# A Fourier block and a gated feed-forward block on one core: half of the last copies put behind the first token products, and one table load moved back in its queue

## The chip, the cores and the metric

The kernel runs on one core of a Trainium2 chip. The metric is the device time of one execution in microseconds, as the median over several runs. A profile comes from one separate, profiled execution, whose own time stands beside it. The engines are called PE (matrix products), ACT, DVE and POOL (element-wise work), and SP, which here only issues transfers. POOL issues transfers as well as computing, and an engine takes its instructions strictly in the order in which they stand in its queue.

## The reference, cut to what matters

The input x has 2048 tokens of 576 features in bf16.

```
def _A_ref(x, w_r, w_i):
    X = rfft2(x.astype(float32), axes=(-2, -1))
    X = X * (w_r + 1j * w_i)
    return irfft2(X, s=(S, D), axes=(-2, -1)).astype(bfloat16)

def _B_ref(x, w_gate, w_up, w_down):            # 576 -> 4608 -> 576
    return (gelu(x @ w_gate) * (x @ w_up)) @ w_down

h  = x + _A_ref(_layernorm(x), w_r, w_i)
h2 = h + _B_ref(_layernorm(h), w_gate, w_up, w_down)
```

The two-dimensional transforms are computed as products with tables of cosines and sines. The second part, three products with 4608 wide weights, is most of the arithmetic.

## The kernel before, in words

Tokens lie as 16 tiles of 128 rows: tile c holds the rows 16p + c. The work has three stretches.

The first stretch loads x, takes the statistics of the first layer norm, and makes the forward transform over the rows into U.

The second stretch runs over 16 groups of frequencies, in an order that is written out by hand in `SEQF` (line 28). For a group i, `st_D` transforms along the features, `st_B` finishes the forward transform, `st_T` multiplies by the filter on DVE, and `st_V` begins the inverse transform on PE. Its result, 256 columns in each of two banks, is copied into the tile V by ACT or DVE, or by one engine for each bank (`VENG`, line 29). The last 32 frequencies of every group, the tail, do not go through `st_V`: `st_R` collects the tails of four groups (a quarter q, from 0 to 3) and makes their inverse in one go. For the quarters 0 to 2 the result goes into RB by one copy and from there, because partitions have to change, by eight small transfers into the tile VR; they are dealt out over the queues of SP and POOL (`r0` to `r2` are their semaphores). For quarter 3 it goes straight from the accumulator into VR by eight copies of 32 partitions, four on ACT and four on DVE. The last group is number 15 (`LAST`), and its product and the tail product of quarter 3 close the stretch: `... V15 R3 v15 r3`. A capital letter is the first half of a product, a small one the second half, with the copies that follow.

The third stretch is ordered by `SEQ` (line 35). `I`/`i` (`i_mm`) is the inverse transform along the features of one token tile c: its first half needs V of every group, its second half V and VR of every group. `E` (`i_ev`) copies the result to GS, `N`/`o` (`n_mm`) makes the last inverse step with the table IT, `a` (`x_add`) adds it to x on DVE, `s`, `q`, `c` take the statistics of the second layer norm, `n` (`norm`, line 885, always with the letter P: on POOL) writes the normalised tile into HN, `u`/`U` (`turn_mm`, line 901) transposes it on PE with the table IDT, `e` copies it to HT, and `G0`, `G1` begin the products with the gate and up weights (`gu_part`, line 935). Only the token tiles 0 to 7 (`NPRE`) are done there. The tiles 8 to 15 are deferred: `def_i` and `def_n` (lines 991 and 1011) do them between the weight products of the first 512 tokens, from the third of these on. A product takes one of four pairs of accumulator banks; which pair is free, and so what a product waits for, comes from a small loop above `i_mm` that replays `SEQ`.

After that the kernel is one long row of weight products: gate and up products for 512 tokens at a time (line 948), then the down products (line 1048).

Transfers are issued by SP and POOL in program order. The loads of tables and of the filter come first on SP, in this order at their end: DT (the table of `i_mm`), IT (512 KB, the table of `n_mm`), IDT (32 KB), then four small filter loads of `w_zero`; behind them stand the VR transfers of the quarters. The first slot of the weights is loaded on SP in twelve parts, `a0` to `a5` and `b0` to `b5`, each behind a `hold`, a wait for the last PE instruction before it in the program (`LOADS`, line 31).

Of the kernel before, what the change touches and what calls it, by code (L numbers as in the profile page):

```python
# [15 lines left out]
NT = 16  # L16
# [14 lines left out]
LOADS = {".I0": "a0 a1 a2 a3 a4 a5", ".N0": "b0", ".i3": "b1", ".o1": "b2", ".N3": "b3", ".o3": "b4 b5", ".i7": "d"}  # L31
# [3 lines left out]
SEQ = """I0 I1 I2 i0 E0S i1 E1S i2 E2A N0 I3 o0 i3 N1 I4 o1 a0 E3S N2 o2 a1 s0A q0 i4 a2 s1A I7 c0 N3 E4S q1 s2D i7 I6 o3 E7A i6 c1 N4 o4 a3 q2 E6A c2 N7 I5 o7 a4 n0P N6 s3A a7 i5 n1P n2P q3 c3 o6 u1 U1 u2 E5A u0 U2 a6 n3P e1A e2D U0 N5 u3 e0A o5 a5 U3 G0 e3D G1""".split()  # L35
# [11 lines left out]
def build_tables():  # L47
# [107 lines left out]
    T["VTAB"] = np.stack([v if k else v.reshape(128, 4, 16, 4).transpose(0, 1, 3, 2).reshape(128, 256) for v, k in ((VN[0, 0], 1), (VN[0, 0], 0), (VN[1, 0], 1), (VN[1, 1], 1), (VN[1, 0], 0), (VN[1, 1], 0))], 1).reshape(128, -1)  # L155
# [176 lines left out]
def _build(nc, A_x, A_w_r, A_w_i, B_w_gate, B_w_up, B_w_down, out):  # L332
# [20 lines left out]
    VR = sb.alloc("VR", [128, NG, 2, 4, NT], BF16)  # L353
# [58 lines left out]
    RB = sb.alloc("RB", [128, 3, 2, 2, 4, NT], BF16)  # L412
# [20 lines left out]
    P.op(POOL, lambda g: g.memset(VR[:, :, :, :, :], 0.0), w=[("V", g, 2 + t) for g in range(NG) for t in range(2)])  # L433
# [51 lines left out]
    P.dma(SP, IT[:, :, :, :].rearrange("p a b c -> p (a b c)"), dram["ITAB"][:, :], "it", w=["IT"])  # L485
    P.dma(SP, IDT[:, :], dram["EYE"][:, :], "eye", w=["IDT"])
# [199 lines left out]
    def st_V(i, second, engs):  # L686
        g, z, b0 = GORD[i], i % NZ, FB["V", i]

        def mm(h, o, ct, first, last, after):
            c, t_ = ct  # L690
            return P.op(PE, lambda t: t.matmul(bank(b0 + o, 0, 128, 128 * c, 128 * c + 128), TP[64 * h:64 * h + 64, z, o, t_, c:256:2], VT[64 * h:64 * h + 64, 0 if g else 2 + o, t_, :],  # L691
                                               start=first, stop=last), r=[("T", z), "VT" if g else "VT2"], w=[("PS", b0 + o)], after=after)

        halves(("V", i), second, [[(c, t_) for c in range(2) for t_ in range(2)]] * 2, mm)
        if not second:
            return
        v5 = V[:, :, :, :, g, :, :].rearrange("p c t n j e -> p j (c t n) e")
        n = 2 // len(engs)
        for a, e in enumerate(engs):
            ev(e, v5[:, n * a:n * a + n], banks(b0 + a, n, 256).rearrange("p a (c e) -> p a c e", e=4), [("PS", b0 + a + k) for k in range(n)], [("V", g, a + k) for k in range(n)])  # L700

    def st_R(q, second):
# [12 lines left out]
        if q < 3:  # L715
            ev(RENG[q], RB[:, q, :, :, :, :].rearrange("p t o e n -> p o t (e n)"), banks(b0, 2, 128).rearrange("p o (t x) -> p o t x", t=2), keys, [("RB", q)])
            for j, i in enumerate(js):
                for t_ in range(2):
                    k = t_ if q == 2 else (2 * j + t_) % 3 > 0
                    P.dma((SP, POOL)[k], VR[64 * t_ + 32 * (j % 2):64 * t_ + 32 * (j % 2) + 32, GORD[i], :, :, :], RB[32 * j:32 * j + 32, q, t_, :, :, :], f"r{q}{k:d}", r=[("RB", q)], w=[("V", GORD[i], 2 + t_)])  # L720
            return
        for i in js:
            j, g = i % 4, GORD[i]
            for t_ in range(2):
                dst = VR[64 * t_ + 32 * (j % 2):64 * t_ + 32 * (j % 2) + 32, g, :, :, :].rearrange("p o e n -> p o (e n)")
                src = PS[32 * j:32 * j + 32, b0 * 512:(b0 + 2) * 512].rearrange("p (a c) -> p a c", a=2)[:, :, 128 * (i == LAST) + 64 * t_:128 * (i == LAST) + 64 * t_ + 64]
                ev((ACT, DVE, DVE, ACT)[j], dst, src, keys, [("V", g, 2 + t_)])
# [36 lines left out]

    def tab2_load():
# [13 lines left out]
    def loads(w):  # L779
        for v in LOADS.get(w, "").split():  # L780
            if v == "d":
                tab2_load()
# [27 lines left out]
    vkeys = vmain + vtail  # L810


    SLOT, last, held, ing = {}, [sorted(used.values()).index(used[2 * b]) - 4 for b in range(4)], set(), False
    for t, w in enumerate(SEQ):
# [6 lines left out]
        elif k in "ioUEae":  # L821
            b = SLOT[{"i": "I", "o": "N", "U": "u", "E": "I", "a": "N", "e": "u"}[k], i] // 2
            if k in "Eae":
                held.discard(b)
            else:
                last[b] = t + 1
        elif k == "G":
# [5 lines left out]
    def i_mm(c, second):  # L833
        b, e = SLOT["I", c], ends.setdefault(("I", c), [None, None])
        for j in range(2 + second):
            for r in range(2):
                o, r0 = r ^ (not second), 64 * r
                lhs = V[r0:r0 + 64, j, o, c, :, :, :] if j < 2 else VR[r0:r0 + 64, :, :, :, c].rearrange("p g o e -> p (g o e)")
# [121 lines left out]
    def gu_first(i):  # L960
        for a in range(4):
# [5 lines left out]
           "e": turn_ev, "G": gu_first}  # L967
# [18 lines left out]
    fdead = ["DT", "IT", "J0", "J1", "ZD"] + [(n_, c) for n_ in ("ATB", "ATS") for c in range(NT)] + [("G", i // 2, i % 2) for i in range(10)] + [*[("Y", a) for a in range(NY)], *[("RB", a) for a in range(3)]]  # L986
# [4 lines left out]
    def def_i(c, second):  # L991
        e = ends.setdefault(("X", c), [None, None])
        for j in range(3):
            for r in range(2):
                o, r0 = r ^ (not second), 64 * r
                t_ = j if j < 2 else r
                lhs, rhs = (V[r0:r0 + 64, o, t_, c, :, :, :], DP[r0:r0 + 64, 2 * o + t_, :]) if j < 2 else (VR[r0:r0 + 64, :, :, :, c].rearrange("p g o e -> p (g o e)"), DP[r0:r0 + 64, 4 + o, :])
                e[o] = P.op(PE, lambda t, o=o, t_=t_, lhs=lhs, rhs=rhs, j=j: t.matmul(bank(6 + o, 0, 128, HK * t_, HK * t_ + HK), lhs, rhs, start=(not second and j == 0), stop=(second and j == 2)),  # L998
                            r=vk[o if j < 2 else 2] + ["DP"], w=[("PS", 6 + o)], after=[e[o]] if second and j == 0 else [])
# [134 lines left out]
```

## Time and profile before

| what | value |
|---|---|
| runs, us | 486.0, 485.41, 485.42; median 485.42 |
| profiled execution: its own time / the span of the instructions | 484.82 us / 483.0 us |
| PE busy | 476.7 us, 99% of the span |
| DVE, ACT, POOL busy | 183.2, 145.4, 51.2 us |
| granted PE clock | full speed in all of the 40 slices |
| gate and up products (lines 948, without and with WGX) | 233.4 + 53.4 us |
| down products (line 1048) | 133.0 us |
| end of the second stretch to the first weight product | 42.2 us to 54.3 us of the span |

The profiled execution is 1.8 us longer than its span; what lies around the span is taken as unchanged. The page counts a matmul as busy until a modelled end, so gaps of PE shorter than about 0.3 us show in the starts of its matmuls more than in its busy time. The stretch that the change touches is short, from about 24 us to 59 us; the 420 us after it are products back to back.

### The profile page before, as it was taken

The numbers are of one execution on the slowest core, as the hardware profiler recorded it, in microseconds if no ns is written. First come the engines' busy times: TensorE is split into PE (matmuls) and PEld (weight loads), VectorE is DVE, ScalarE is ACT, GpSimd is POOL, SyncE is SP. The second block draws the span as 40 slices with busy tenths as digits, with TensorE's granted clock in tenths as the row PEclk, the third lists the DMA queues.
The fourth block names the chain that finished last, engine by engine and source line by source line (L and its number), as shares of the span: only waits on it lengthen the run. The fifth ranks groups of instructions, "written<-read, shape, count | busy, mean of one in ns | idle before, by whom it ended". The sixth has DMA issues, their size and how long they took to land.

```text
span 483.0 us, 12887 instructions
## 1 busy us (share of the span) xinstructions
PE 476.7 (99%) x5873; PEld 289.0 (60%) x5874; DVE 183.2 (38%) x366; ACT 145.4 (30%) x291; POOL 51.2 (11%) x86
## 2 busy tenths in 40 slices
PE   7999999999999999999999999999999999999998
PEld 3877755555588644444688544444788444445884
DVE  7998655565500143333200244333101233333011
ACT  6998753434300022332100122233000232223000
POOL 7753317010120000000000000000000000000000
PEclk9999999999999999999999999999999999999999
DMA  8883878951520001000000011000000000000000
GB/s 292 226 219 70 278 248 289 375 104 27 195 88 17 26 18 23 18 1 0 3 14 15 26 24 23 12 0 2 3 14 27 14 1 0 1 1 1 3 26 26
DMA packets 28454, 33.19 MB, mean 69 GB/s; under 512 B 12656, under 2 KB 21488, under 8 KB 28400
## 3 DMA queue, kind: packets, MB, share of 16 engines
q1 hardware_dynamic: 24768, 19.88, 14.6%
q0 software_dynamic: 3632, 12.49, 7.9%
q8 instruction: 46, 0.75, 0.7%
q14 instruction: 8, 0.07, 0.0%
HBM read 26.21 MB, written 2.36 MB: 59 GB/s over the span
## 4 chain that ended last, share of the span: by engine, by line
PE 96%; DVE 1%; DMA 1%; POOL 1%; issue 0%; SPq 0%; POOLq 0%; DVEq 0%
PE PS L948 58%; PE PS L1048 27%; PE PS L650 2%; PE PS L1060 2%; PE PS L691 2%; PE PS L561 1%; DMA XO<-in_A_x_dram 1%; PE PS L670 1%; PE PS L839 1%; PE PS L998 1%; DVE XO L862 1%; PE PS L1015 0%; PE PS L856 0%; POOL XN L577 0%; POOL ATS L530 0%
## 5 line engine op out<-in xcount | busy, mean ns | idle before, releaser
L948 PE MATMUL PS<-HT,WG 64*128 64x512 bf16 (+1 forms) x2142 | 233.4, 372 | 0.1
L948 PEld LDWEIGHTS PS<-HT,WG 64*128 64x128 bf16 x2142 | 109.2, 94 | 111.1 <-DMA WG<-in_B_w_up_dram 0.2
L956 ACT ACTIVATE GL<-PS 128x512 bf16<-128x512 f32 x144 | 85.7, 596 | 281.8 <-PE PS L948 281.8
L957 DVE TENSOR_TENSOR AT<-GL,PS 128x512 bf16<-128x512 bf16 x144 | 98.8, 687 | 166.0 <-ACT GL L956 166.0
L1048 PE MATMUL PS<-WD,AT 64*128 64x288 bf16 x2160 | 133.0, 283 | 0.0
L1048 PEld LDWEIGHTS PS<-WD,AT 64*128 64x128 bf16 x2160 | 107.9, 94 | 25.2
L1035 DVE TENSOR_TENSOR OS<-PS,XO 128x288 bf16<-128x288 f32 (+2 forms) x32 | 13.2, 452 | 125.5 <-PE PS L1048 118.0
L948 PE MATMUL PS<-HT,WGX 64*128 64x512 bf16 x486 | 53.4, 376 | 0.0
L948 PEld LDWEIGHTS PS<-HT,WGX 64*128 64x128 bf16 x486 | 24.3, 94 | 28.2
L865 ACT ACTIVATE OS<-XO,NM 128x576 bf16<-128x576 bf16 x15 | 11.6, 773 | 11.4 <-DVE XO L1019 11.4
L650 PE MATMUL PS<-FT,U 64*128 64x288 bf16 x160 | 13.3, 283 | 0.0
L683 DVE TENSOR_TENSOR TP<-YS,WS 128x1024 bf16<-128x1024 bf16 x16 | 11.0, 686 | 0.9 <-DMA WS<-WS 0.6
L504 DVE BATCH_NORM_STATS2 ST<-XO 128x6 f32<-128x288 bf16 x26 | 10.1, 440 | 2.0 <-DMA XO<-in_A_x_dram 2.0
L691 PE MATMUL PS<-VT,TP 64*128 64x128 bf16 x256 | 10.0, 217 | 0.0
L242 POOL DMA_DIRECT2D WG<-in_B_w_gate_dram x9 | 6.1, 679 | 34.4 <-DMA WG<-in_B_w_gate_dram 31.0
L572 ACT ACTIVATE U<-PS 128x384 bf16<-128x384 f32 (+2 forms) x27 | 9.4, 485 | 0.7 <-PE PS L561 0.7
L561 PE MATMUL PS<-ATS,XO 128*128 128x128 bf16 x96 | 8.1, 219 | 1.5 <-POOL ATS L530 1.5
L242 POOL DMA_DIRECT2D WD<-in_B_w_down_dram x9 | 6.7, 755 | 23.8 <-PE PS L1015 23.8
L616 ACT ACTIVATE CUS<-PS 128x576 bf16<-128x576 f32 x14 | 9.0, 656 | 0.3 <-PE PS L650 0.2
L1060 PE MATMUL PS<-WD,AT 128*128 128x448 bf16 (+1 forms) x72 | 9.0, 286 | 0.0
L616 ACT ACTIVATE YS<-PS 128x576 bf16<-128x576 f32 x14 | 8.9, 657 | 0.3
L691 PEld LDWEIGHTS PS<-VT,TP 64*128 64x128 bf16 x256 | 7.9, 94 | 1.4 <-DVE V L616 0.2
(89 smaller groups left out, 227.9 us busy)
## 6 DMA issues: line engine op xcount, KB each, us to landing
WD<-in_B_w_down_dram POOLq DMA_DIRECT2D x9, 576.0 KB, 12.1
WG<-in_B_w_up_dram SPq DMA_DIRECT2D x6, 576.0 KB, 7.1
WG<-in_B_w_gate_dram POOLq DMA_DIRECT2D x6, 576.0 KB, 6.3
out_dram<-OS SPq DMA_DIRECT2D x30, 72.0 KB, 1.7
XO<-in_A_x_dram SPq DMA_DIRECT2D x6, 288.0 KB, 4.8
WGX<-in_B_w_up_dram SPq DMA_DIRECT2D x2, 576.0 KB, 4.4
WGX<-in_B_w_gate_dram POOLq DMA_DIRECT2D x2, 576.0 KB, 5.5
HT<-HN SPq DMA_TRANSPOSE x60, 2.4
```

Of the source, the lines that this page charges most:

```text
L242: fn = lambda e: e.dma_start(out_ap, in_ap)
L561: P.op(PE, lambda t, b=b, lhs=lhs, p0=p0, p1=p1, s=s, e=e, o=o, c=c: t.matmul(bank(b, p0, p1, o, o + 128), lhs, ATS[:, c, :], start=s, sto ...
L616: fn = (lambda v: v.tensor_copy(dst, src)) if eng == DVE else (lambda a: a.activation(dst, src, ACTF.Copy))
L650: return P.op(PE, lambda t: t.matmul(bank(b0 + o, 0, 128, 0, 2 * HK), U[64 * h:64 * h + 64, us, 2 * i:2 * i + 2, :, :], FT[64 * h:64 * h + ...
L691: return P.op(PE, lambda t: t.matmul(bank(b0 + o, 0, 128, 128 * c, 128 * c + 128), TP[64 * h:64 * h + 64, z, o, t_, c:256:2], VT[64 * h:64 ...
L865: P.op(ACT, lambda a, c=c, out=out: a.activation(out, XO[:, c, 0:D], ACTF.Square, bias=NM[:, c:c + 1], accum_out=SB2[:, 1, c:c + 1]), r=[( ...
L948: op = P.op(PE, lambda t, h0=h0, kt=kt, wt=wt, b=b, s=(not second and j == 0), e=(second and j == n - 1): t.matmul(bank(b, 0, 128, c0, c1) ...
L956: P.op(ACT, lambda a: a.activation(GL[:, s2, :], bank(b0), ACTF.Gelu_apprx_tanh), r=[("PS", b0)], w=[("GL", s2)])
L957: P.op(DVE, lambda v: v.tensor_tensor(AT[:, f, :], GL[:, s2, :], bank(b0 + 1), op=ALU.mult), r=[("GL", s2), ("PS", b0 + 1)], w=[("AT", f)])
L1035: P.op(DVE, lambda v: v.tensor_tensor(OS[:, p % 2, d0:d1], bank(b, 0, 128, 0, d1 - d0), XO[:, c, d0:d1], op=ALU.add), r=[("PS", b), ("X", ...
L1048: e[h] = P.op(PE, lambda t, f=f, h=h, r0=r0, j=j: t.matmul(bank(b0 + h, 0, 128, 0, 288), AT[r0:r0 + 64, f, 128 * p:128 * p + 128], WD[r0:r ...
L1060: P.op(PE, lambda t, b=b, d0=d0, d1=d1, f=f, j=j: t.matmul(bank(b, 0, 128, 0, d1 - d0), AT[:, f, 128 * p:128 * p + 128], WD[:, f, d0:d1], ...
```

## The change

There are four edits.

1. The copies that close the second stretch are cut in two by token tiles. The token index of V and VR is split into tiles 0 to 7 and tiles 8 to 15. For group 15 (`v_half`) each engine first copies the half for tiles 0 to 7, 128 columns in place of 256. For quarter 3 the eight copies into VR take 64 columns in place of 128, the tiles 0 to 7. The other half of group 15 is copied by the new entry `l15`, which stands behind `i0`. The other half of quarter 3 is copied by the new entry `l3` (`tail_late`), behind `I3`: one copy of 96 partitions on ACT and one of 32 partitions on DVE into RB, and then eight transfers of 4 KB from RB to VR, all on the queue of POOL (semaphore `rl`). The products of the deferred tiles wait for all of these; those of the tiles 0 to 7 wait only for the first halves.
2. `SEQ` changes at its head: `I2` moves behind `i0`, since its banks are those of group 15, which are held until `l15`. The bank loop counts the banks of group 15 and of quarter 3 as held until `l15` and `l3`.
3. The loads of IT and IDT leave their place in front of the four loads of `w_zero` and stand on SP behind the VR transfers of quarter 1 (`"r1": "t"` in `LOADS`).
4. VR gets a layout with the two halves of the tiles apart, so a transfer writes two runs of 64 elements to a partition in place of one of 128. The 24 transfers of the quarters 0 to 2 are dealt out anew: SP issues 5, 5 and 4 of them and POOL 3, 3 and 4, where it was 3, 3, 4 and 5, 5, 4. One table has its columns in another order to match.

```diff
-LOADS = {".I0": "a0 a1 a2 a3 a4 a5", ...
+LOADS = {"r1": "t", ".I0": "a0 a1 a2 a3 a4 a5", ...
-SEQ = """I0 I1 I2 i0 E0S i1 E1S i2 E2A N0 I3 o0 i3 N1 I4 o1 a0 E3S ...
+SEQ = """I0 I1 i0 l15 E0S I2 i1 E1S i2 E2A N0 I3 l3 o0 i3 N1 I4 o1 a0 E3S ...
...
-    VR = sb.alloc("VR", [128, NG, 2, 4, NT], BF16)
+    VR = sb.alloc("VR", [128, 2, NG, 2, 4, NT // 2], BF16)
...
-    P.dma(SP, IT[:, :, :, :].rearrange("p a b c -> p (a b c)"), dram["ITAB"][:, :], "it", w=["IT"])
-    P.dma(SP, IDT[:, :], dram["EYE"][:, :], "eye", w=["IDT"])
...
+        if i == LAST:
+            v_half(i, 0, ("V", g))
+            return
...
+    def v_half(i, k, key):
+        for a, e in enumerate((ACT, DVE)):
+            src = bank(FB["V", i] + a, 0, 128, 0, 256).rearrange("p (q x) -> p q x", q=4)[:, :, 32 * k:32 * k + 32].rearrange("p q (n e) -> p q n e", e=4)
+            ev(e, V[:, :, :, 8 * k:8 * k + 8, GORD[i], a, :].rearrange("p c t n e -> p (c t) n e"), src, [("PS", FB["V", i] + a)], [(*key, a)])
...
-                    k = t_ if q == 2 else (2 * j + t_) % 3 > 0
+                    k = t_ ^ (j % 2) if q == 2 else (2 * j + t_) % 3 == 1
...
+    def tail_late(q, engs):
+        b0 = FB["R", 3]
+        for p0, p1, c, e in ((0, 96, 0, engs[0]), (96, 128, 128, engs[1])):
+            ev(ENG[e], RB[p0:p1, 0, :, 1, :, :].rearrange("p t o x -> p o t x"), PS[p0:p1, b0 * 512:(b0 + 2) * 512].rearrange("p (a c) -> p a c", a=2)[:, :, c:c + 128].rearrange("p a (t x) -> p a t x", t=2)[:, :, :, 32:64],
+               [("PS", b0), ("PS", b0 + 1)], [("RB", 0, p0)])
+        for i in range(12, 16):
+            for t_ in range(2):
+                j = i % 4
+                P.dma(POOL, tail_place(i, t_, 1), RB[32 * j:32 * j + 32, 0, t_, 1, :, :].rearrange("p o x -> p (o x)"), "rl", r=[("RB", 0, 96 if i == LAST else 0)], w=[("VL", GORD[i], 2 + t_)])
...
+    def it_load():
+        P.dma(SP, IT[:, :, :, :].rearrange("p a b c -> p (a b c)"), dram["ITAB"][:, :], "it", w=["IT"])
+        P.dma(SP, IDT[:, :], dram["EYE"][:, :], "eye", w=["IDT"])
...
+    vlate = [("VM", GORD[LAST], a) for a in range(2)] + [("VL", GORD[i], 2 + t) for i in range(12, NG) for t in range(2)]
...
-                            r=vk[o if j < 2 else 2] + ["DP"], w=[("PS", 6 + o)], after=[e[o]] if second and j == 0 else [])
+                            r=(vk[o] if j < 2 else vtail) + vlate + ["DP"], w=[("PS", 6 + o)], after=[e[o]] if second and j == 0 else [])
```

41 lines of the change are left out of this document (23 added, 18 removed).

## The prediction

> **What bounds the kernel now.** I read the page first: PE is busy for 99% of the span at the full clock, and the chain that ended last is PE for 96% of it. So almost all of the time is products the change does not touch, and it can only act through the moment at which the weight products begin. Then I read the chain of waits from the end of the second stretch to that moment.
>
> ```profile
> 42.17 0.42 DVE V L616
> 42.60 0.14 issue
> 42.73 1.16 PE PS L839 x16
> 43.89 0.06 issue
> 43.95 1.08 PE PS L839 x14
> ...
> 45.86 0.76 DVE XO L862
> ...
> 50.19 0.67 DVE XO L862
> 50.86 0.05 issue
> 50.91 0.42 PE PS L839 x4
> ...
> 54.27 0.06 issue
> 54.33 0.70 PE PS L948 x9
> ```
>
> PE waits for the copy of group 15 into V (to 42.73), then for the copies into VR (to 43.95), later for DVE's additions (to 50.91), and the weight products begin at 54.33. Next the timelines of DVE and POOL.
>
> ```profile
> 42.16 0.42 DVE L616 CAST V<-PS 128x256 bf16<-128x256 f32 x1
> 42.62 1.19 DVE L616 CAST VR<-PS 32x128 bf16<-32x128 f32 x4
> ...
> 39.23 1.96 POOL L242 DMA_DIRECT2D VR<-RB  x4 [0.27 <-ACT RB L616]
> 48.64 0.86 POOL L890 TENSOR_SCALAR HN<-XO,NM,RS 128x640 bf16<-128x640 bf16 x1 [7.45 <-DVE RS L875]
> 50.30 0.87 POOL L890 TENSOR_SCALAR HN<-XO,NM,RS 128x640 bf16<-128x640 bf16 x1 [0.80 <-DVE RS L875]
> 51.34 0.87 POOL L890 TENSOR_SCALAR HN<-XO,NM,RS 128x640 bf16<-128x640 bf16 x1 [0.17 <-POOL HN L890]
> 52.54 0.87 POOL L890 TENSOR_SCALAR HN<-XO,NM,RS 128x640 bf16<-128x640 bf16 x1 [0.32 <-DVE RS L875]
> ```
>
> The reader is to see two things: DVE's copies on the path are half a microsecond and less, and POOL, which looks idle from 41.2 to 48.6, makes the four normalised tiles of the first 512 tokens one behind the other until 53.41. PE transposes the last of them from 53.61 on, 0.20 us after POOL ends, and 0.7 us later the weight products begin. Last the transfers.
>
> ```profile
> IT<-c_itab SPq DMA_DIRECT2D x1, 512.0 KB, 6.1
> VR<-RB SPq DMA_DIRECT2D x10, 8.0 KB, 3.0
> WG<-in_B_w_up_dram SPq DMA_DIRECT2D x1, 112.0 KB, 6.3
> ```
>
> The last weight part leaves SP at 52.01 and lands 6.3 us later, at 58.3. The 72 matmuls with the first 256 weight columns run from 54.33 with one start every 0.055 us, to 58.3 as well. So starting them earlier, without earlier weights, brings nothing.
>
> **The front (edits 1 and 2).** DVE's copies of 256 and 512 columns take 0.42 and 0.68 us, so a column costs 0.001 us: 128 columns 0.29, 64 columns about 0.22 (an estimate from these rows; the 128-column VR copies take 0.285). PE starts 0.13 earlier, at 42.60. I0, I1 and i0 are 12 matmuls at 0.061 a start, to 43.34. The VR copies, four at 0.22 with 0.014 between them from 42.48, end at 43.41, and PE starts 0.15 after such an end (42.58 to 42.73 in the rows): 43.56, where it was 43.95. But now I2 has still to come (0.25 us), and it waits for DVE's second half of group 15, 0.29 us behind the VR copies: 43.71, PE at 43.86. So i1 begins at 44.10, before it was 44.11: nothing is left. Then a small loss: I3 now takes the banks of token 1, whose copies on DVE end at 45.13, so it starts at 45.28, where it stood at 45.16. That moves DVE's first addition from 45.86 to 45.98, and DVE has no gap from there to 50.86. The front is worth between -0.13 (the start alone) and +0.12; I take +0.12 at 50.9, and it stays behind what follows. The l3 copies cost about 0.27 (ACT) and 0.29 (DVE), in gaps of 0.53 and 0.73 us in front of ACT's 46.25 and DVE's 45.86; without that cover they would add that much.
>
> **POOL's eight new transfers (edit 1).** ACT's l3 copy runs behind the copy that ends at 45.72, to 45.93. POOL started its transfers of quarter 2 0.29 us after the copy they read (38.95 to 39.23), so here at 46.2. It issues one in 0.49 us (x4 in 1.96), whatever DVE does meanwhile (DVE was 100% busy from 39 to 41): eight take 3.9 us, to 50.1. The four normalisations are queued behind them. They take 0.87 with 0.17 between two: they end at 51.0, 52.1, 53.1 and 54.1, where they ended at 49.5, 51.2, 52.2 and 53.4. The first two are not yet awaited: PE transposes tile 1 from 52.26. Tile 2 reaches PE at 53.30 in place of 52.7, tile 3 at 54.34 in place of 53.61. What follows tile 3 is o5, U3 and the weight products: 0.44 us of starts and about 0.1 more, so 54.87. Before, the last 0.2 us went to ACT's copy of tile 0, which now ends at 54.7 and is not last. The weight products start +0.54 late. Bounds: a POOL issue at the dearest row of its kind, 0.59 us for the filter copies at 32.3, adds 8 x 0.10 = 0.8; with normalisations without a gap it is 0.4 less. I take the middle, since the VR rows are the nearest.
>
> **The weights.** They hang on SP's holds; the first is for I0, about 0.13 earlier. They land at 58.2 to 58.6 (the 32 KB of late VR data are 0.1 us at the 280 GB/s worked out below; up to 0.3 if their small packets cost more), before PE needs them at 58.8. The 0.05 us that PE may lose to them now is gone.
>
> **The tables on SP (edits 3 and 4).** Four w_zero loads leave 0.96 us earlier (two issues of 0.44 with their steps). POOL's filter copies waited 2.67 us for one of them to 32.3, and DVE waited 0.45 and 0.20 us for such copies; PE stands back to back there, so I count nothing, between -0.4 and 0. SP issues five r1 transfers from 33.89 (0.5 to 0.6 each, one of 1.25 as in every quarter) to 37.6, IT and IDT to 38.55, and reaches r2 at 38.97, as before. IT, by its 6.1 us, is there by 43.8, and its first reader comes at 44.9; IDT's comes at 52.3. The r2 transfers now stand behind 544 KB: they landed by 43.4 and are needed at 43.5. At 280 GB/s, which the b parts show (448 KB every 1.6 us), IT's data take 1.9 us and are gone by about 41.6, so the last two, issued at 40.2 and 41.5, land as before. Runs of 128 bytes in place of 256 double small packets and I count nothing for them, at most 0.1 us. The wait on rl before the deferred products costs nothing: the last lands by 52.7 (1.6 to 2.6 after issue on POOL), they start at 60.5.
>
> **Sum.** +0.54 - 0.05 = +0.5 us. On the profiled execution's 484.82 that is 485.3. The median of the runs is 0.6 above it, at 485.42; the same step gives 485.9.
>
> **Rivals.** (1) Slower by more than a measurement can tell: r2 lands late. In the trace r0, with the queue full, took 4.6 us to land and more, r2 with it empty 2.4 to 3.0. If the full-queue price holds for the last r2 transfer, or r2 waits for IT's 6.1 us (43.8 to 44.2, plus their own time), the products with VR start at 44.6, 1.05 late, and so does l3 with POOL's row behind it: +0.5 + 1.0, 486.9. It decides once the last r2 lands after 43.5. Against it: small w_i loads issued at 25.58, behind IT, landed at 29.2, before IT's 30.7. [...] (2) POOL's issues cost 0.59 or more: +0.5 + 0.8 = +1.3, 486.7. (3) POOL's row is hidden, as when its issues overlap or PE finds other work: then the front decides, from 0.13 earlier to 0.12 later, and weights that land at 58.2 cap the gain: 485.3. With up to 0.4 from the earlier filter copies, 485.0.
>
> **How the numbers follow.** A change under 0.2% (0.97 us) can hardly be told from none. Forecast 0.60, rival 1 0.12, rival 2 0.12, rival 3 0.16. The forecast is inside the bound but for 0.03 of its chance on the slow side, rivals 1 and 2 are outside on the slow side in all but 0.02, rival 3 is inside but for 0.03 on the fast side. So faster 0.03, same 0.72, slower 0.25. The likeliest alone lies between 485.5 and 486.3; the range runs from rival 3's front case to rival 1, with 0.1 for the spread of runs: 485.1 to 486.9.
>
> **What would show it.** In the profile after: PE's first V product near 42.6 and its first VR product near 43.55; a wait of PE before I2 and before I3; eight POOL issues from 46.2 to 50.1 and the normalisations shoulder to shoulder behind them, the last ending near 54.1; PE waiting for HN between 52.8 and 54.3; the first weight product near 54.9. I am wrong if POOL's row does not delay the last normalisation, if the first VR product waits for a transfer, or if the second stretch itself changes length by more than 0.3 us.

## The result, and the profile after

The changed kernel takes 488.79 us (median of 11 executions, 487.26 to 489.77). The kernel before, run beside it, takes 485.75 us (11 executions, 484.95 to 486.97). The ratio is 1.0056, with a 95% interval from 1.0042 to 1.0070. So it is slower by about 2.7 us by the ratio (3.0 between the medians), where the forecast was +0.5 with a range up to +1.5.

The profiled execution has a span of 486.9 us (before 483.0) and its own time is 488.72 us. From the third weight product to the end the kernel takes 424.8 us (before 424.7), so the whole loss lies in front of it. The chain of waits of the changed kernel (start, duration, what), from the transfers of quarter 2 to the first weight product, with the numbers of its own lines (L866 is `i_mm`, L883 `n_mm`, L889 `x_add`, L935 `turn_mm`, L975 the weight products):

```profile
40.31 0.60 SPq L242
40.90 0.04 issue
40.95 3.77 DMA VR<-RB
44.71 0.46 issue
45.17 1.40 PE PS L866 x18
46.57 0.48 PE PS L883 x4
47.05 0.48 PE PS L866 x4
...
50.04 1.49 DVE XO L889 x2
...
53.27 0.66 DVE XO L889
53.94 0.05 issue
53.98 0.42 PE PS L866 x4
...
57.34 0.77 DVE XO L889
58.11 0.14 issue
58.24 6.31 PE PS L975 x92
```

Three things are new in it. The first VR product starts at 45.17 (before 43.95) and waits for a transfer of quarter 2 that was issued at 40.95 and landed at 44.71; that is one of the signs by which the prediction wanted to be called wrong. From 46.57 on, four products take 0.48 us, where most rows of four of before have 0.24 to 0.26. And the first weight product, at 58.24 in place of 54.33, waits for an addition of DVE that ends at 58.11. The waits of PE (us in total, times, longest) say the same:

```profile
PE PS L866 <- DMA VR<-RB: 2.0, 1, 2.0
PE PS L975 <- DVE XO L889: 0.9, 1, 0.9
```

Next the timelines of DVE and POOL after the change (start, us, work, idle time before it and what ended that):

```profile
42.13 0.92 DVE L614 CAST VR<-PS 32x64 bf16<-32x64 f32 x4
43.08 0.29 DVE L614 CAST V<-PS 128x128 bf16<-128x128 f32 x1
...
47.71 3.94 POOL L242 DMA_DIRECT2D VR<-RB  x8 [6.71 <-ACT RB L614]
51.72 0.87 POOL L917 TENSOR_SCALAR HN<-XO,NM,RS 128x640 bf16<-128x640 bf16 x1
53.38 0.87 POOL L917 TENSOR_SCALAR HN<-XO,NM,RS 128x640 bf16<-128x640 bf16 x1 [0.80 <-DVE RS L902]
54.43 0.88 POOL L917 TENSOR_SCALAR HN<-XO,NM,RS 128x640 bf16<-128x640 bf16 x1 [0.17 <-POOL HN L917]
55.62 0.88 POOL L917 TENSOR_SCALAR HN<-XO,NM,RS 128x640 bf16<-128x640 bf16 x1 [0.31 <-DVE RS L902]
```

The eight new issues take 3.94 us, as forecast, but 1.5 us later, and the second and the last normalisation wait for DVE's RS, as they did before: DVE is so late here that the row on POOL decides nothing. The transfers between 38 and 47 us (bytes each, median time from issue to landing):

```profile
IT<-c_itab SPq DMA_DIRECT2D x1, 512.0 KB, 3.9
...
VR<-RB POOLq DMA_DIRECT2D x4, 8.0 KB, 2.9
VR<-RB SPq DMA_DIRECT2D x4, 8.0 KB, 3.2
```

The transfers of VR in the same stretch of before, and one window of 3.41 us of before (busy time of PE, PEld, DVE, ACT and POOL, granted clock, DMA share, GB/s):

```profile
VR<-RB POOLq DMA_DIRECT2D x6, 8.0 KB, 1.9
VR<-RB SPq DMA_DIRECT2D x4, 8.0 KB, 2.7
```

```profile
42.88:46.29 3.41, 3.35 (x54) 2.56 (x52) 2.13 (x7) 2.08 (x7) 0.00 (x0) 1.00 0.47 124
```

Three windows of the same length after, the first in the same place:

```profile
42.88:46.29 3.41, 1.40 (x24) 1.15 (x20) 1.07 (x4) 0.86 (x4) 0.00 (x0) 1.00 0.60 159
46.29:49.70 3.41, 3.41 (x33) 2.67 (x30) 1.72 (x4) 2.03 (x5) 1.99 (x5) 0.50 0.47 126
49.70:53.11 3.41, 3.30 (x50) 2.13 (x46) 3.07 (x5) 2.41 (x8) 2.82 (x5) 1.00 0.89 274
```

After the window with the wait, in which PE was busy for 1.40 of 3.41 us (before 3.35), the granted clock is 0.50 for 3.41 us, and then full again. Of the 11 executions three kept the full clock throughout (487.26, 487.32 and 487.37 us); eight had a mean granted clock of 0.996 or 0.997 and took 487.92 to 489.77, with a median of 488.88.

So the 3.91 us by which the first weight product is late are made up, in the profiled execution, of -0.49 (PE's first V product at 42.24, before 42.73), +1.71 (from there to the VR product, 2.93 in place of 1.22) and +2.69 (from there to the first weight product, 13.07 in place of 10.38). The experiments take these apart.

### The profile page after: what moved, and what is told of

Same layout as the page of the kernel before. It is cut to its first block, busy times and chain, and to the rows that moved or that the text cites. A ratio compares the mean times of both kernels' runs of the same rounds, so it can differ in the third digit from the quotient of the medians.

```text
span 486.9 us, 12902 instructions
## 1 busy us (share of the span) xinstructions
PE 478.3 (98%) x5874; PEld 342.7 (70%) x5874; DVE 184.0 (38%) x368; ACT 145.5 (30%) x293; POOL 52.8 (11%) x90
## 4 chain that ended last, share of the span: by engine, by line
PE 94%; DMA 1%; POOL 1%; DVE 1%; ACT 1%; issue 1%; SPq 0%; POOLq 0%; DVEq 0%
PE PS L975 58%; PE PS L1075 27%; PE PS L1087 2%; PE PS L648 2%; PE PS L559 1%; PE PS L866 1%; DMA VR<-RB 1%; PE PS L689 1%; DMA XO<-in_A_x_dram 1%; PE PS L883 1%; PE PS L1025 1%; DVE XO L889 1%; PE PS L668 1%; ACT YS L614 1%; POOL XN L575 0%
## 5 line engine op out<-in xcount | busy, mean ns | idle before, releaser
L975 PE MATMUL PS<-HT,WG 64*128 64x512 bf16 (+1 forms) x2142 | 233.7, 372 | 0.9 <-DVE XO L889 0.9
L975 PEld LDWEIGHTS PS<-HT,WG 64*128 64x128 bf16 x2142 | 131.1, 94 | 90.4 <-issue 1.0
L1075 PEld LDWEIGHTS PS<-WD,AT 64*128 64x128 bf16 x2160 | 132.3, 94 | 0.7
L975 PE MATMUL PS<-HT,WGX 64*128 64x512 bf16 x486 | 53.6, 376 | 0.0
L975 PEld LDWEIGHTS PS<-HT,WGX 64*128 64x128 bf16 x486 | 29.9, 94 | 22.5
L242 POOL DMA_DIRECT2D VR<-RB x18 | 9.2, 521 | 11.1 <-ACT RB L614 11.1
```

Source lines behind the costliest of these rows:

```text
L242: fn = lambda e: e.dma_start(out_ap, in_ap)
L975: op = P.op(PE, lambda t, h0=h0, kt=kt, wt=wt, b=b, s=(not second and j == 0), e=(second and j == n - 1): t.matmul(bank(b, 0, 128, c0, c1) ...
L1075: e[h] = P.op(PE, lambda t, f=f, h=h, r0=r0, j=j: t.matmul(bank(b0 + h, 0, 128, 0, 288), AT[r0:r0 + 64, f, 128 * p:128 * p + 128], WD[r0:r ...
```

## The experiments

All times are ratios to the kernel before, run on the same chip beside each, with 95% intervals. "V", "VR" and "first weight product" are starts on PE in the profiled execution.

### The late transfers: one table move, one dealing

**The table move alone**: the kernel before with edit 3.

```diff
-LOADS = {".I0": "a0 a1 a2 a3 a4 a5", ".N0": "b0", ".i3": "b1", ".o1": "b2", ".N3": "b3", ".o3": "b4 b5", ".i7": "d"}
+LOADS = {"r1": "t", ".I0": "a0 a1 a2 a3 a4 a5", ".N0": "b0", ".i3": "b1", ".o1": "b2", ".N3": "b3", ".o3": "b4 b5", ".i7": "d"}
-    P.dma(SP, IT[:, :, :, :].rearrange("p a b c -> p (a b c)"), dram["ITAB"][:, :], "it", w=["IT"])
-    P.dma(SP, IDT[:, :], dram["EYE"][:, :], "eye", w=["IDT"])
...
+    def it_load():
+        P.dma(SP, IT[:, :, :, :].rearrange("p a b c -> p (a b c)"), dram["ITAB"][:, :], "it", w=["IT"])
+        P.dma(SP, IDT[:, :], dram["EYE"][:, :], "eye", w=["IDT"])
```

> The kernel before with edit 3 alone: IT and IDT behind the transfers of quarter 1 on SP. Theory A: r2 lands after 44, PE's first VR product moves from 43.95 to about 45, the kernel is 1 us slower, and 1.5 us more in executions where the clock drops (ratio 1.002 to 1.005). Theory B: r2 lands by 43.4 as before, no change beyond 0.2 us (ratio 1.000).

Measured: 485.16 us, ratio 0.9996 (0.9987 to 1.0005), all ten executions at full clock. IT is issued at 35.94 and landed at 39.91. The last r2 lands at 43.19 and VR starts at 43.76, the first weight product at 54.14. So the table move by itself neither costs nor gains, as theory B has it: an early r2, as before, and a start 0.19 us earlier, which a later wait of 0.9 us for a weight part takes back.

**Everything but the table move**: the changed kernel with edit 3 undone.

```diff
-LOADS = {"r1": "t", ".I0": "a0 a1 a2 a3 a4 a5", ".N0": "b0", ".i3": "b1", ".o1": "b2", ".N3": "b3", ".o3": "b4 b5", ".i7": "d"}
+LOADS = {".I0": "a0 a1 a2 a3 a4 a5", ".N0": "b0", ".i3": "b1", ".o1": "b2", ".N3": "b3", ".o3": "b4 b5", ".i7": "d"}
...
+    P.dma(SP, IT[:, :, :, :].rearrange("p a b c -> p (a b c)"), dram["ITAB"][:, :], "it", w=["IT"])
+    P.dma(SP, IDT[:, :], dram["EYE"][:, :], "eye", w=["IDT"])
```

> The changed kernel with edit 3 alone undone: IT and IDT are loaded again in front of the filter loads of w_zero; the copies in halves, the late row on POOL, the new layout and the new dealing stay. Theory A (the r2 transfers are late because they stand behind IT and IDT in SP's queue): r2 lands by about 43.4, PE waits less than 0.3 us before the first VR product instead of 2.0, the granted clock stays full, and what is left over the kernel before is the row on POOL and the wait of the first weight product for the last addition, about +1.5 us (ratio 1.003). Theory B (r2 is late because its transfers have twice as many runs and are dealt out anew): nothing changes, the wait stays at 2 us and the ratio near 1.0056.

Measured: 487.16 us, ratio 1.0041 (1.0027 to 1.0056), six executions at full clock (486.68 to 487.43) and two below it (488.33, 488.37). IT landed at 31.35, the last r2 lands at 43.89, and VR starts at 44.35, behind a wait of 0.5 us where theory A allowed 0.3. Most of the loss is still there, though r2 is only half a microsecond late. So r2 is not the only cause; the wait of 0.88 us in front of the first weight product is here too (56.38).

**The old dealing**: the changed kernel with SP 3, 3, 4 and POOL 5, 5, 4 transfers, as before.

```diff
-                    k = t_ ^ (j % 2) if q == 2 else (2 * j + t_) % 3 == 1
+                    k = t_ if q == 2 else (2 * j + t_) % 3 > 0
```

> The changed kernel with the dealing of the 24 tail transfers as it was (SP 3, 3, 4 and POOL 5, 5, 4); tables behind quarter 1, halves, layout and the late row on POOL stay. Theory F (neither edit alone but both: five transfers of quarter 1 on SP instead of three hold IT back by about 2 us, so that its data run into r2's): IT leaves SP near 36 and not near 38, r2 lands about 0.9 us after PE's first V product (2.5 in the changed kernel), the first VR product follows 0.46 us behind that, the clock drops in few executions or none, and the kernel is 1.0 to 1.5 us slower than the one before (ratio 1.002 to 1.003). Theory G (the halved runs and the layout make r2 late by themselves once a table is near): r2 still lands 2 us or more after the first V product and the ratio stays above 1.004.

Measured: 486.88 us, ratio 1.0032 (1.0020 to 1.0044), seven executions at full clock and three below. With two r1 transfers fewer on SP, IT is issued at 36.71 in place of 37.92, and that is enough: r2 lands at 43.22, and VR starts at 43.67. What remains is the forecast's row on POOL, to the tenth, and a wait behind it that the forecast did not have. From the chain of waits of this kernel:

```profile
50.12 0.88 POOL HN L917
...
51.17 0.88 POOL HN L917
...
52.21 0.89 POOL HN L917
...
53.26 0.89 POOL HN L917
54.14 0.14 issue
54.28 0.26 PE PS L935 x6
54.54 0.26 PE PS L883 x4
54.80 0.02 issue
54.83 0.77 DVE XO L889
55.59 0.14 issue
55.73 4.33 PE PS L975 x45
```

The normalisations end at 51.0, 52.1, 53.1 and 54.1. The weight products could start at 54.85 (forecast 54.87), but wait 0.88 us for DVE's last addition. This execution is one of the three below full clock; the half clock comes late in it, from 55.95 to 59.36, so that the third weight product follows the first after 5.59 us in place of 3.93.

**Table or dealing**: two runs for the question that these three leave open, whether IT's data do it, the five transfers on SP, or the order inside SP's queue. In the first the changed kernel keeps its dealing and loads IT behind quarter 0. In the second it has the old dealing, and IT stands behind the first r2 transfer on SP.

```diff
-LOADS = {"r1": "t", ".I0": "a0 a1 a2 a3 a4 a5", ".N0": "b0", ".i3": "b1", ".o1": "b2", ".N3": "b3", ".o3": "b4 b5", ".i7": "d"}
+LOADS = {"r0": "t", ".I0": "a0 a1 a2 a3 a4 a5", ".N0": "b0", ".i3": "b1", ".o1": "b2", ".N3": "b3", ".o3": "b4 b5", ".i7": "d"}
```

```diff
-LOADS = {"r1": "t", ".I0": "a0 a1 a2 a3 a4 a5", ".N0": "b0", ".i3": "b1", ".o1": "b2", ".N3": "b3", ".o3": "b4 b5", ".i7": "d"}
+LOADS = {".I0": "a0 a1 a2 a3 a4 a5", ".N0": "b0", ".i3": "b1", ".o1": "b2", ".N3": "b3", ".o3": "b4 b5", ".i7": "d"}
...
                     k = t_ if q == 2 else (2 * j + t_) % 3 > 0
...
+                    if (q, j, t_) == (2, 0, 0):
+                        it_load()
```

> The changed kernel with IT and IDT behind the transfers of quarter 0 in place of those of quarter 1; the dealing of 5, 5 and 4 on SP stays. IT is then issued near 33.8, and its data are gone by about 38, before r2 begins. Theory (r2 is late because IT's data move while r2 is under way): the last r2 lands at 43.2 to 43.9, PE's first VR product 0.46 later, the time 1.003 to 1.004 of the kernel before, as with the old dealing (486.5 to 487). Rival (five and five on SP make r2 late, whatever IT does): the last r2 lands near 44.7 and the time stays at 1.0055.

> The changed kernel with the old dealing (3, 3 and 4 on SP), and IT and IDT issued behind the first of the four r2 transfers on SP, so near 39.3 to 40.3. POOL's four r2 transfers are issued from 38.9 to 41.0 as ever, on a queue that holds nothing of the tables. Theory (IT's data hold up whatever is under way beside them): POOL's last r2 lands at 44.3 or later where it landed at 42.88 with the old dealing, SP's at 44.7 or later, VR near 45.2, time 1.005 or more. Rival (the order within SP's queue does it): POOL's last lands at 42.9, and only SP's three come late.

Measured, first: 487.14 us, ratio 1.0038 (1.0025 to 1.0051); the last r2 lands at 43.25 and VR starts at 43.71, with the new dealing. Second: 488.33 us, ratio 1.0059 (1.0040 to 1.0078); SP's last r2 lands at 44.99, POOL's last at 44.31, VR starts at 45.45. The transfers of the second from 38.5 us on:

```profile
IT<-c_itab SPq DMA_DIRECT2D x1, 512.0 KB, 4.7
...
VR<-RB SPq DMA_DIRECT2D x4, 8.0 KB, 2.4
VR<-RB POOLq DMA_DIRECT2D x4, 8.0 KB, 3.3
```

and the same stretch of the first, with IT's data gone before:

```profile
VR<-RB SPq DMA_DIRECT2D x4, 8.0 KB, 2.6
VR<-RB POOLq DMA_DIRECT2D x4, 8.0 KB, 2.0
```

So r2 is late where IT's data move while it is under way, on whichever queue it stands: POOL's four, issued from 38.9 to 41.0 on a queue that holds no table, take 3.3 us in place of 2.0. The dealing matters in the changed kernel only because it holds IT back by 1.2 us. In the packets of the changed kernel the last 128 bytes of r2 start at 42.97 us and the semaphore comes 1.7 us later, at 44.71; with the old dealing the last starts at 42.86 and lands at 43.22.

The lateness hangs on a few updates. The trace has 16 updates of the semaphore for each transfer. Of the 64 for SP's four r2 transfers in the changed kernel, 60 had come by 43.39, where the kernel with the table behind quarter 0 had all 64 by 43.25; the last four came at 43.67, 44.19, 44.53 and 44.71. In that kernel and with the old dealing one packet of 16 KB with instructions moves from 40.09 to 41.05 and from 40.01 to 41.00; in the changed kernel it moves from 41.31 to 42.25, directly behind IT's data. Whether this packet, the first weight packets at 43.75 or something else holds the last four updates isn't shown.

### The wait in front of the weight products

**Other banks**: the changed kernel, with two products on each other's banks. The bank loop takes the pair that was used longest ago; since `SEQ` and the held banks have changed at the head, everything behind them rotates. The last two `N` products and `I5` have other pairs than before, and the first weight product finds its pair held by `a5`, the last addition.

```diff
-            b = min((b for b in range(2 * ing, 4) if b not in held), key=lambda b: last[b])
+            b = {"I5": 0, "N6": 3}.get(w, min((b for b in range(2 * ing, 4) if b not in held), key=lambda b: last[b]))
```

> The changed kernel with one choice of accumulator banks forced: I5 takes pair 0 and N6 pair 3, so that N5 lies in pair 3 and not in pair 0, which the first weight product needs. Theory C (the rotation of the banks that edit 2 brought makes the first weight product wait for the addition a5): PE's wait of 0.9 us before the first weight product goes, the product starts about 0.8 us earlier against the same point (end of U3), and the time falls by 0.7 to 0.9 us (ratio to the kernel before 1.004 instead of 1.0056). Rival: another wait ends just as late there (the copy of tile 0, or the weights, which land at 58.4), and less than 0.2 us is gained.

Measured: 487.63 us, ratio 1.0046 (1.0021 to 1.0070). The wait for the addition is gone, and two for the normalisations stand in its place:

```profile
PE PS L867 <- DMA VR<-RB: 2.3, 1, 2.3
PE PS L936 <- POOL HN L918: 0.6, 2, 0.5
```

The first weight product starts 14.25 us after V in place of 16.00, with a VR product as late as in the changed kernel (45.43) and, in the profiled execution, the full clock. Since the trace of the changed kernel has the half clock in this stretch, only a part of these 1.75 us is the bank's. Kernels with the old choice of banks and the full clock between VR and the first weight product need 12.04 us for that stretch (those with the table inside the last quarter and with the zeros below, where VR is as late, and three others); here it is 11.07. That makes the bank 0.97 us. Half of the ten executions fell below full clock, and the interval is too wide to tell the time from that of the changed kernel.

**Old dealing and other banks together**: the changed kernel with both edits.

```diff
-                    k = t_ ^ (j % 2) if q == 2 else (2 * j + t_) % 3 == 1
+                    k = t_ if q == 2 else (2 * j + t_) % 3 > 0
...
-            b = min((b for b in range(2 * ing, 4) if b not in held), key=lambda b: last[b])
+            b = {"I5": 0, "N6": 3}.get(w, min((b for b in range(2 * ing, 4) if b not in held), key=lambda b: last[b]))
```

> The kernel of the run before this one with I5 forced into bank pair 0 and N6 into pair 3 as well, so that the first weight product does not wait for the last addition. What is left is the row of eight transfers on POOL: the normalisations end near 1.6 us later than in the kernel before relative to the first V product, PE waits 0.5 to 0.9 us for HN, and the first weight product comes 12.0 to 12.4 us after the first V product (11.6 in the kernel before). Ratio 1.000 to 1.002. If the banks were no separate cost, no change against the run before.

Measured: 485.95 us, ratio 1.0011 (1.0002 to 1.0021), no execution below full clock. Against the old dealing alone that is 0.0021 of 485 us, 1.0 us, for a wait of 0.88 and the clock that three of ten lost there. PE's waits are now those for the normalisations:

```profile
PE PS L936 <- POOL HN L918: 0.7, 2, 0.5
```

The first weight product starts 12.16 us after V, before 11.60: +0.56. From VR it is 11.09 us, as with the other banks alone (11.07), before 10.38.

### The row on POOL

**The eight transfers behind the normalisations**: the kernel just shown, with the issues of `rl` in an entry `L3` behind `n3P`.

```diff
-SEQ = """... u0 U2 a6 n3P e1A e2D U0 ...
+SEQ = """... u0 U2 a6 n3P L3 e1A e2D U0 ...
...
                [("PS", b0), ("PS", b0 + 1)], [("RB", 0, p0)])
+
+    def tail_send(q):
         for i in range(12, 16):
             for t_ in range(2):
...
-           "e": turn_ev, "G": gu_first, "l": ...
+           "e": turn_ev, "G": gu_first, "L": tail_send, "l": ...
```

> The same with the eight late transfers issued behind the four normalisations on POOL instead of in front of them. Theory H (the row on POOL delays the normalisations): PE's waits for HN go, the normalisations end as in the kernel before, and the first weight product comes 11.5 to 11.8 us after the first V product; the last of the eight lands after 59, so the first deferred product (6.2 us behind the first weight product) may wait up to 1 us for it. Ratio 0.999 to 1.002. Rival (the normalisations wait for DVE anyway): no change against the run before.

Measured: 485.44 us, ratio 1.0000 (0.9991 to 1.0009), no execution below full clock. The normalisations end at 49.49, 51.16, 52.21 and 53.54 (before 49.50, 51.17, 52.22 and 53.41), and the waits for them are gone. Two small ones are new:

```profile
PE PS L869 <- ACT GS L614: 0.3, 1, 0.3
...
PE PS L1028 <- DMA VR<-RB: 0.2, 1, 0.2
```

The first is the price of the chosen banks (`I5`), the second that of the late transfers in the deferred products; the last of these lands at 60.92. The first weight product comes 12.04 us after V, where 11.5 to 11.8 were expected: from VR it is 10.83 us, so that only 0.26 of the 0.71 us that the row cost come back in front of the weight products, and 0.4 us are lost again behind the third of them. That the row delays the normalisations is shown by their ends; what moving it is worth is 0.5 us by the runs, with intervals that overlap, and less by the trace. So the steps from 1.0056 are 1.0032, 1.0011 and 1.0000, and with three causes undone the change is worth nothing. VR starts at 43.67, 0.28 earlier than before, and the first weight product at 54.50, 0.17 later.

### The clock

**Zeros in the wait**: the changed kernel with 20 products of a zero tile in front of the VR products.

```diff
+            for _ in range(20 if (c, j) == (0, 2) else 0):
+                P.op(PE, lambda t: t.matmul(bank(...), ZD[:, 0:128], ZD[:, 0:224], start=False, stop=False), ...)
```

> The changed kernel with 20 matmuls of zeros (224 columns, about 0.093 us each, 1.9 us) put on PE just before the first VR product, into columns that nobody reads, so that PE is busy through most of its wait for r2. Theory D (the half clock from 46.3 to 49.7 comes from PE's 2 us of idleness): the granted clock stays full in all executions, matmuls of the stage come every 0.061 us again, and the time falls to that of the executions with full clock, 487.3, about 1.5 us less (ratio 1.003). Rival (the drop has another cause, such as the load of the second stretch): the clock still drops in most executions and the time stays near 488.8.

Measured: 488.92 us, ratio 1.0072 (1.0049 to 1.0095); of four executions two at full clock (488.34, 488.41) and two below (489.44, 490.22). Nothing follows: the products outlasted the wait by 0.3 us, later waits of 0.5 and 0.9 us remain in the kernel, and whether products of zeros do for the clock what others do isn't shown.

**A made wait in the kernel before**: copies of a dead scratch tile on POOL behind r2, for which the first VR product waits. A twin, with `range(20)` in place of `range(0)`, fills the wait with 20 products of the table DT into columns that nobody reads.

```diff
+            if (c, j) == (0, 2):
+                for _ in range(5):
+                    late = [P.op(POOL, lambda g: g.tensor_scalar(JNK[:, 1, :], JNK[:, 0, :], 1.0, 1.0, ...))]
+                for _ in range(0):
+                    P.op(PE, lambda t: t.matmul(bank(...), DT[:, 0, 0:128], DT[:, 1, 0:224], ...))
```

> The kernel before, with five copies of a dead scratch tile (128x576, about 0.8 us each) on POOL behind the last r2 transfer, and the first VR product waits for the last of them. Nothing else of the change is in it. PE then idles about 2 us in front of the VR products (they start near 46 in place of 43.95), as it does in the changed kernel, with transfers that land on time. Theory (a wait of about 2 us lets the granted clock fall for 3.4 us): the executions fall into two groups, one about 2 us above the kernel before (487.5 to 488), and one, a third or more of all, about 1.5 us above that (489 to 489.5). Rival (the fall has to do with the late transfers or with the later waits of the change): one group, near 487.8, no slice under full clock.

> As in the run with the idle time alone, with 20 matmuls of 224 columns on the data of the table DT in PE's wait, into columns that nobody reads (0.093 us each, 1.9 us together, so PE is busy for nearly all of the wait). Theory (it is the idleness that lets the clock fall): one group, at the time of the lower group of the run without them, 487.5 to 488, no execution under full clock. Rival (the lateness itself or something else does it): two groups as there, a third or more of the executions near 489 to 489.5.

Measured: 486.65 us, ratio 1.0026 (1.0017 to 1.0035), ten executions, and 487.15 us, ratio 1.0029 (1.0016 to 1.0041), six executions, all at full clock. The pair misses its question. In the profiled execution the second stretch ended 1.7 us later than in that of before (V at 44.41), so that PE waited only 0.4 us for the copies. The 20 products of the twin take 2.02 us, 0.101 us each.

**The same, later**: four copies, started only by PE's first V product (`first`).

```diff
-                for _ in range(5):
-                    late = [P.op(POOL, lambda g: g.tensor_scalar(JNK[:, 1, :], JNK[:, 0, :], 1.0, 1.0, ...))]
+                for _ in range(4):
+                    late = [P.op(POOL, lambda g: g.tensor_scalar(JNK[:, 1, :], JNK[:, 0, :], 1.0, 1.0, ..., after=first))]
...
+                first.append(e[o]) if not first else None
```

> As the first run with a made wait, but with four scratch copies on POOL that start only behind PE's first V product (42.7), so that they no longer run beside DVE's last copies of the second stretch, and at 0.75 us each end near 45.9. PE idles about 2 us in front of the VR products (start 46.0 in place of 43.95); all transfers land on time and nothing of the change is in the kernel. Theory (a wait of about 2 us lets the granted clock fall for 3.4 us): the first weight product 2.0 later, and the executions in two groups, near 487.3 and, a third or more of all, near 488.8. Rival (the fall needs what else the change does): one group near 487.3.

> As that run, with 20 matmuls of 224 columns on the data of the table DT in the wait (0.101 us each as measured, 2.0 us together). Theory: one group, near 487.3, none under full clock; rival: a third or more of the executions near 488.8, as without the matmuls.

Measured without filling: 488.35 us, ratio 1.0062 (1.0039 to 1.0086); two executions at full clock, 487.42 and 487.60, and two below it, 489.10 and 489.27. With filling: 487.63 us, ratio 1.0056 (1.0041 to 1.0071), all four at full clock, 487.44 to 488.48. The windows of the unfilled one:

```profile
44.71:48.12 3.41, 1.44 (x22) 1.22 (x24) 0.83 (x2) 1.05 (x3) 1.66 (x3) 1.00 0.65 173
48.12:51.53 3.41, 3.36 (x30) 2.11 (x26) 1.63 (x3) 1.79 (x5) 0.00 (x0) 0.50 0.61 154
51.53:54.94 3.41, 3.33 (x50) 2.20 (x50) 3.21 (x8) 2.48 (x7) 1.20 (x2) 1.00 0.90 299
```

and the filled wait of the other:

```profile
43.88:46.82 2.94, 2.80 (x34) 2.29 (x28) 0.67 (x3) 0.45 (x2) 2.67 (x4) 1.00 0.45 112
```

A wait of 2.3 us, with nothing of the change in the kernel, is followed by the same half clock for 3.41 us, behind a window with PE busy for 1.44 us of it. From VR to the first weight product it is 11.96 us there and 10.37 with the wait filled, as before (10.38): the half clock costs 1.58 us. Four executions without a fall prove little alone. With all runs: kernels with an unfilled wait of 2 us or more fell below full clock in 17 of 29 executions (changed kernel 8 of 11, other banks 5 of 10, table inside the last quarter 2 of 4, made wait 2 of 4). Those with the wait of 0.9 us in front of the weight products, and the shorter ones before it, fell in 6 of 24 (old dealing 3 of 10, table in front 2 of 8, table behind quarter 0 1 of 6), and the rest, the zeros left aside, never. The cleanest pair is other banks against old dealing and other banks together, which differ in the dealing alone and, by it, in r2's lateness: 5 of 10 executions fell against 0 of 10. The counts do not say behind which wait an execution fell. In the kept traces of the old dealing and of the table inside the last quarter it is in the first weight products (from 55.95 and 57.59), behind windows with PE busy for 1.87 and 1.82 us; the second of these kernels has a wait of 2.3 us for r2 and came through that at full clock.

### The other direction

**The last tables in front**: the kernel before with edit 3, and DP and ITD, the tables of the deferred products, loaded behind the last weight part.

```diff
-LOADS = {"r1": "t", ".I0": "a0 a1 a2 a3 a4 a5", ".N0": "b0", ".i3": "b1", ".o1": "b2", ".N3": "b3", ".o3": "b4 b5", ".i7": "d"}
+LOADS = {"r1": "t", ".I0": "a0 a1 a2 a3 a4 a5", ".N0": "b0", ".i3": "b1", ".o1": "b2", ".N3": "b3", ".o3": "b4 b5 d"}
```

> The kernel before with edit 3 alone, and with the tables of the deferred tiles (DP, ITD, 472 KB) loaded behind the last weight parts instead of in front of them. Theory I (the table move alone shortens the second stretch by 0.2 to 0.4 us, and the weights, which landed 5.0 us after the first weight product there, took it back): the wait of 0.9 us before the third weight product goes, and the kernel is 0.3 to 0.6 us faster than before (ratio 0.9988 to 0.9994). Rival (the weights are not the limit in most executions): ratio 0.9996 as with the table move alone.

Measured: 485.22 us, ratio 1.0000 (0.9990 to 1.0009). The wait of 0.9 us for a weight part that the table move alone had is gone, and the 0.3 to 0.6 us that were expected of it did not come. No kernel of this study beats the one before by more than a measurement can tell.

## Why the prediction was wrong, by its own steps

**The step that failed** is in "the tables on SP": r2 "landed by 43.4 and are needed at 43.5", and "IT's data take 1.9 us and are gone by about 41.6, so the last two ... land as before". The working of it held: SP stood within 0.3 us of the forecast (r1 to 37.88, r2 from 39.03), and IT's data moved between 39.1 and 41.3. The conclusion did not. The r2 transfers landed later although the data were gone before they should end: 3.2 and 2.9 us in the median in place of 2.7 and 1.9, the last one 3.77 us. The prediction's "2.4 to 3.0" for r2 leaves out that last one on SP, which took 1.80 us before (41.55 to 43.35). The runs of 128 bytes double the packets on SP's queue alone: 64 for an r2 transfer there in place of 32, and 16 of 512 bytes on POOL's in both kernels. What came is rival 1, given a chance of 0.12 and a time of 486.9. Its condition ("once the last r2 lands after 43.5") was right, its landing (43.8 to 44.2 and a little more) too early by half a microsecond.

**The need was mis-stated as well.** VR starts 0.46 us behind the last landing in every kernel where that decides: 44.71 to 45.17, 44.97 to 45.43, 43.89 to 44.35, 43.73 to 44.19, 43.22 to 43.67, 43.25 to 43.71. So the transfers were needed at 43.1 for a start at 43.56, not at 43.5. It also means that before the change they already stood close behind DVE's copies (43.34 + 0.46 = 43.80, against 43.95): the halved copies of quarter 3, the heart of edit 1, could gain 0.15 us at most in front of the VR products.

**Not in the working at all**: that held banks rotate all later ones. The forecast followed the rotation for `I2` and `I3`, and not to the end, where the first weight product got the pair of `a5`. That is a wait of 0.89 us in the changed kernel, and of 0.88 in those with the table in front and with the old dealing; undoing it was worth 0.97 us from VR to the first weight product.

**Not in the working either**: that a wait of 2 us can cost more than itself. The executions of the changed kernel below full clock take 1.56 us longer in the median than those at full clock (488.88 against 487.32), and they are 8 of 11, so it is in the median. In the kept trace the half clock accounts for 1.03 us (the sum below); what else parts the two groups no trace shows. The half clock stands in that trace from 46.29 to 49.70, 3.41 us, and by the counts it comes in some executions and not in others. In the 3.41 us ahead of it PE was busy for 1.40 us, with the made wait for 1.44, and with the old dealing, where three short waits lie in them, for 1.87. How little work of PE brings it isn't shown.

**What was right.** The row of eight issues on POOL: 46.14 to 50.07 in the kernel with the old dealing (forecast 46.2 to 50.1), the last normalisation at 54.14 (54.1), the weight products ready at 54.85 (54.87). That the times agree to the tenth is in part luck: V starts 0.32 earlier there than forecast, VR 0.11 later, and with the other banks the whole row stands 0.5 later. In that kernel, where the row is what is left, the runs have 0.0011 of 485 us, 0.5 us (+0.54). That rival 2's dear issue did not come: 0.49 us each. DVE's copies: 0.22 and 0.28 to 0.30 us (0.22 and 0.29). The front as a whole worth nothing: in the kernel with the old dealing DVE's first addition starts at 45.85, before 45.86 (forecast 45.98). The weights land in time: the third weight product follows the first after 3.93 us, before 4.02. **Mis-sized**: V starts 0.49 earlier in place of 0.13. The remaining 0.36 lies in the second stretch and inside the bound given there (-0.4 to 0, from the earlier filter copies). DVE's two waits for such copies (0.45 and 0.20 us) are gone from the trace, but the length of the stretch scatters by as much between the kernels, so its cause isn't shown.

**The sum, as the runs have it.** In the profiled execution: -0.49 at the front, +1.71 for r2 (it takes back that gain and 1.22 more), +1.66 for row and bank, +1.03 for the half clock: +3.91. Row and bank are read from kernels at full clock: from VR to the first weight product those with neither need 10.38 us, the two with the row alone 11.07 and 11.09, the five with both 12.04 to 12.06. What the changed kernel's 13.07 has beyond 12.04 is put down to the half clock. In the kernel with the made wait it cost 1.58; here it makes DVE so late that the row is not awaited any more, so the two prices do not add up. Of the large terms the forecast had the row alone.

## What to carry to other kernels

Before shortening the copies in front of a wait, see what else that wait hangs on and by how much it would be next: here transfers stood 0.15 us behind the copies. See whether a large load moves while small transfers that a product waits for are under way, on their queue or on another: here 512 KB issued 1.2 us later made the last of them 1.5 us late, and POOL's took 3.3 us in place of 2.0 with the load on SP. When an edit changes which accumulator banks are held, follow the rotation to the end of the written order; and look at the granted clock behind a new wait of PE: here executions with one of 2.0 to 2.3 us fell below full clock in 17 of 29, which cost another 1.0 and 1.6 us in the two kept traces that have the fall behind that wait.

## What the runs showed of the hardware that was not expected

- Kernels in which PE waits for 2.0 to 2.3 us fell below full clock in 17 of 29 executions, in the kept traces to half for 3.41 us. That cost 1.0 us (changed kernel) and 1.6 us (made wait). In the traces of the changed kernel and of the made wait it begins 1.1 and 1.4 us after PE is back at work. With 20 products of the table DT in the made wait it did not come (0 of 4); with products of zeros in the wait of the changed kernel 2 of 4 fell.
- From the landing of the last of the r2 transfers to the first product that waits for it are 0.455 to 0.46 us on PE, in eight kernels; from the end of a DVE copy it is 0.14.
- POOL's issue of a transfer with two runs to a partition takes 0.533 us (table inside the last quarter) to 0.536 us (changed kernel), with one run 0.496 to 0.498; at the head of a row both can take up to 0.03 us more.
- The semaphore of a small transfer came up to 1.7 us after the start of its last packet when IT's 512 KB had ended 1.7 us before that packet (changed kernel), against 0.34 to 0.38 us in the kernel before, with the old dealing and with the table behind quarter 0.
